# One kernel, two stored orders: attention and a SwiGLU layer on one core, with spare matmuls in other waits

## The chip, the cores and the metric

The kernel runs on one core of a Trainium2 chip. A core has five engines with a queue of instructions each: TensorE (PE, matrix products), VectorE (DVE), ScalarE (ACT), GpSimd (POOL) and SyncE (SP, which here only issues transfers). They run side by side and wait for each other through semaphores; transfers (DMAs) are issued from the queues of SP, ACT and POOL. Matrix products go to PSUM, a small memory that DVE and ACT read, and that POOL doesn't; everything else that is at hand lies in SBUF. The metric is the time of one execution in microseconds, the median of several runs.

## The reference

Attention with a forgetting factor, and a feed-forward layer (FFN) on its output:

```python
scores = scale * np.matmul(q, k.transpose(0, 1, 3, 2))        # 8 batches, 8 heads, 576 tokens, 64 wide
log_f = np.log(np.clip(f, 0.0001, 1.0))
cum = np.cumsum(log_f, axis=-1)
decay = cum[:, :, :, None] - cum[:, :, None, :]
scores = np.where(causal, -1000000000.0, scores + decay)
attn = softmax(scores)                                        # with 1e-09 in the divisor
x = np.matmul(attn, v)                                        # -> 4608 tokens x 512
xn = x / np.sqrt(np.mean(x * x, -1) + 1e-06) * rms_g
g, val = xn @ w_gate, xn @ w_val                              # 512 -> 1536, twice
out = (g * sigmoid(g) * val) @ w_out                          # 1536 -> 512, float32
```

The decay is split into a factor of the query, which the softmax's division removes, and one of the key, exp(-cum), by which the kernel scales the rows of V and a column of ones beside them.

## The kernel before, in words

**Pieces.** The program is cut into 1,551 pieces. Each has a name, an engine, a function that emits its instructions, and the pieces and buffers that it needs. A stored string, ORDER, lists the names; `plan.run` emits the pieces in exactly this order. So ORDER fixes two things: the order of the instructions in each engine's queue (an engine executes its own queue strictly in order, so a piece that waits holds up all that stand behind it on that engine), and which buffer a piece gets when it takes one, since a buffer must have been released by a piece that stands earlier. A word in ORDER may carry marks: `@A`, `@D`, `@O`, `@S` put the piece on ACT, DVE, POOL or SP where there is a choice, `:ff` takes a product's PSUM buffer from the FFN's pool, and `*n` asks for n spare matmuls ahead of the piece.

**Spare matmuls.** They multiply a zeroed 128x128 tile, `idle`, with itself, into the PSUM buffer that the piece has just taken and is about to overwrite. They wait for that buffer, and for nothing that the piece reads. Their result is never used:

```python
def warm_up(ps):                                   # L248 to L253
    k = st.pop("fill", 0)
    for w in [4] * (k // 4) + [1] * (k % 4):
        ...
        nc.tensor.matmul(ps[:, 0:w * 128], lhsT=idle, rhs=x, start=True, stop=True)
```

Score banks with masked blocks are opened by a piece of their own, `far`, which writes large negative numbers where a key lies behind the query; the score piece that follows finds the bank open:

```python
sc = T["sc", b, p, c0] if ("sc", b, p, c0) in T else open_sc(p, c0)    # scores(); open_sc calls warm_up
st.pop("fill", 0)
```

**Stages.** For each batch b: `L` pieces load q, k and v in pieces of 256 KB (Lq0.1 is the second part of batch 0's q; Lqk00 and Lqk01 are the last 64 tokens of q and k, half a piece each; Lv0.40 and Lv0.41 those of v, a quarter each), from SP's queue or ACT's. `C` pieces cast q and k to bfloat16 on POOL, ACT or DVE (L222). For batches 0 to 2 PE turns them (`tr`, `trt`, into a PSUM buffer of the FFN's pool, L528 to L558), and `keeptr` copies move them into QK or QT on DVE or ACT; for the later batches a transposing DMA on SP's queue does it (`tk`, `tq`, `tt`, L592 and L595). `S` pieces scale V by the decay (L451 to L458), which waits for `keep_dec`, the copy of the decay factors. Then for each pair p of heads: score banks (`sc`, L679; batch 0 has smaller banks than the others, and the masked ones begin with `far`, L664), exponentials on ACT (`esc`, L688), masks on POOL (L694), products with V (`val`, L714), division on DVE (`xpo`, L721 and L722). `sc4`, `exp4` and `mask4` are the last 64 keys. Row sums of squares on ACT (`sq`, L729), the inverse root on POOL (`rs`, L735), the norm on DVE (`xn`, L739), and a transpose of x on PE for batches 0 and 1 (`xtr`, L766), by DMA on SP's queue for the others (`tx`, L758).

**FFN.** The 4,608 tokens form ten groups, two of 256 and eight of 512. For each group and each 128 of the 1,536 columns PE computes a gate product (`g`) and a value product (`v..f`), four matmuls each (L863); ACT takes tanh of the gate (`th`, L868), DVE joins them in two steps (`ga` L872, `hga` L879). The output product (`pj`, L889) is copied out (`o`, L222) and stored (`so`, L897) from POOL's, SP's or ACT's queue. The FFN of earlier tokens is interleaved with the attention of later ones, so that PE has work while ACT computes exponentials.

**Buffers.** PSUM has two score banks ("sc"), one product buffer ("po") and three for everything else ("ff"). Ten staging buffers hold loads until they are cast.

**The front.** Weights are cast while they are loaded, from POOL's queue (`wg0` to `wv2`, L381; `wo`, L393). ORDER begins with constants, the log and the running sum of f, batch 0's loads and the first spare matmuls, and comes to the first FFN product, g0.0, after some 180 pieces.

Of the kernel before, what the change touches and what calls it, by code (L numbers as in the profile page):

```python
# [26 lines left out]
Cq1.0 Lv0.3 keeptr0.10.k Cqk0@D far0.2.0 keeptr0.10.q sc0.2.0 Lk1.3@A Sv0.0@O trt0 esc0.2.0 Lv0.41 keeptrt0 wv0 sc0.1.1024*6 Cqk1@A val0.0.0 Lk1.2
val0.4.0:ff keep_rg val0.6.0:ff xpo0.0.0 k4.0 Lk1.1 esc0.1.1024 val0.2.0:ff sc0.0.384 Lq1.2 wg0 xpo0.2.0 esc0.1.384 Lq1.1 sc4.0 xpo0.4.0 wg1 exp4.0
xpo0.6.0 esc0.3.384 far0.3.1024*4 esc0.0.384 Ck1.0 esc0.2.384 sc0.3.1024 Sv0.2 sq0.0 sc0.1.512 Lv1.41 trt1 esc0.3.1024 keeptrt1 Lv1.40 Sv0.3@O
esc0.1.512 Lqk20 sc0.0.512*9 Sv0.4 Lqk21 sq0.1 far0.0.1024*2 wv1 sc0.0.1024 esc0.0.512 rs0.0 Lk2.0 esc0.0.1024 sc0.2.512*6 tr1.0 mask4.0 xn0.1  # L30
far0.2.1024 keeptr1.0.q@A k4.1 Lv1.0 sc0.2.1024 esc0.2.512 keeptr1.0.k@D val0.0.2 val0.1.2:ff xpo0.0.2 esc0.2.1024 sc0.3.512 Cq1.2@O xpo0.1.2 val0.2.2
xn0.0 Ck1.1 esc0.3.512 val0.5.2:ff val0.3.2:ff xpo0.5.2 xtr0.0 wg2 sc1.0.512 Cq1.1@A kxtr0.0 xpo0.3.2 esc1.0.512 xtr0.1 Cq1.3 val0.4.2:ff xpo0.2.2
val0.6.2:ff wv2 Lq2.0 xpo0.4.2 kxtr0.1 val0.7.2 xpo0.6.2 Ck1.3@O tr1.1 esc1.0.0 xpo0.7.2 sc4.1 Ck1.2 g0.0 Lv1.3 keeptr1.1.k@D sq0.2 keeptr1.1.q v0.0f
th0.0 sq0.3 ga0.0 g0.2 exp4.1 sq0.4 hga0.0 sc1.0.1024 th0.2 rs0.2 tr1.3 esc1.1.512 ga0.2 xn0.2 v0.2f*4 keeptr1.3.q@A keeptr1.3.k@D esc1.0.1024 g0.4
# [931 lines left out]
```

## Time and profile before

| what | value |
|---|---|
| median of 7 runs | 384.2 us (380.27 to 385.13) |
| profiled execution | 384.62 us, its span 382.9 us |
| PE busy | 365.5 us, 95% of the span |
| DVE, ACT, POOL busy | 260.6, 220.7, 136.2 us |
| chain that ended last, by engine | PE 72%, DMA 8%, issue 6%, DVE 5%, ACT 4%, POOL 3% |
| granted TensorE clock | 0.50 from 21.80 to 28.63 us, 1.00 otherwise |
| first FFN product | 36.97 us |

Busy time of PE is the union of its matmuls' spans, whose ends are modelled, so 95% busy isn't 95% of what PE could do. The span counts from the first instruction to the last; the execution's time has some 1.7 us more. The granted clock is the share of the full clock that the chip's throttle let through; the profile names the stretches.

### The profile page before, as it was taken

The page shows a single profiled execution, that of the slowest core. Times are in us where ns is not written, and L with a number is a line of the kernel's source. Part 1 is how long each engine was busy: PE and PEld are TensorE (multiplying, and loading weights), DVE is VectorE, ACT ScalarE, POOL GpSimd, SP SyncE. Part 2 cuts the span into 40 slices and gives each one's busy share as a digit, 9 for nine tenths or more (in the row PEclk, how much of TensorE's full clock was granted, in tenths as well). Part 3 has the DMA queues.
Part 4 walks back from the last instruction along what each step waited for, and adds up shares of the span by engine and source line. Part 5 has one row for each costly group of instructions (what it writes and reads, how often), then busy time and mean ns, then how long its engine had stood idle before and what let it go on. Part 6 is the DMA issues. An engine that isn't in the chain of part 4 may idle for free.

```text
span 382.9 us, 8139 instructions
## 1 busy us (share of the span) xinstructions
PE 365.5 (95%) x3103; PEld 195.0 (51%) x3144; DVE 260.6 (68%) x497; ACT 220.7 (58%) x369; POOL 136.2 (36%) x249
## 2 busy tenths in 40 slices
PE   7679999999999899999899999999999999999996
PEld 3447788553644544455454544454445544444443
DVE  4648888778867778668757765778467876763560
ACT  5578978578697477544755587346565422323311
POOL 3566293237368144623531564020830111000001
PEclk9969999999999999999999999999999999999999
DMA  9999999697699799979969994641400234002002
GB/s 216 245 249 216 237 197 211 119 230 135 139 229 174 176 172 166 213 153 156 169 160 188 147 198 108 138 99 41 76 35 9 64 82 124 3 0 82 29 0 110
DMA packets 144774, 52.58 MB, mean 137 GB/s; under 512 B 128188, under 2 KB 141120, under 8 KB 144736
## 3 DMA queue, kind: packets, MB, share of 16 engines
q1 hardware_dynamic: 126992, 37.64, 52.1%
q0 software_dynamic: 6016, 8.79, 10.9%
q10 hardware_dynamic: 11728, 5.65, 6.2%
q8 instruction: 24, 0.39, 0.5%
q14 instruction: 14, 0.11, 0.1%
HBM read 37.90 MB, written 9.44 MB: 124 GB/s over the span
## 4 chain that ended last, share of the span: by engine, by line
PE 72%; DMA 8%; issue 6%; DVE 5%; ACT 4%; POOL 3%; SPq 1%; POOLq 0%; ACTq 0%; DVEq 0%
PE ff L863 42%; PE ff L889 18%; DMA st<-in_q_dram 5%; PE sc L679 4%; PE po L714 3%; DMA QK<-ld 2%; DVE xn L739 1%; DMA out_dram<-ores 1%; ACT PT L688 1%; PE ff L714 1%; POOL PT L694 1%; DVE X L722 1%; POOL rs L735 1%; ACT th L868 1%; ACT junk L729 1%
## 5 line engine op out<-in xcount | busy, mean ns | idle before, releaser
L868 ACT ACTIVATE th<-ff 128x512 f32<-128x512 f32 x108 | 64.5, 598 | 92.9 <-PE ff L863 88.2
L863 PE MATMUL ff<-xT,wv 128*128 128x512 bf16 (+1 forms) x466 | 109.7, 357 | 1.5 <-DVE ga L872 0.8
L863 PE MATMUL ff<-xT,wg 128*128 128x512 bf16 (+1 forms) x464 | 109.3, 357 | 0.8
L688 ACT ACTIVATE PT<-sc 128x1024 bf16<-128x1024 f32 (+2 forms) x100 | 96.4, 991 | 15.7 <-PE sc L679 13.8
L872 DVE SCALAR_TENSOR_TENSOR ga<-th,ff 128x512 f32<-128x512 f32 x108 | 74.0, 686 | 42.0 <-ACT th L868 41.5
L889 PE MATMUL ff<-wo,hT 128*128 128x512 bf16 (+1 forms) x433 | 97.4, 373 | 0.8 <-issue 0.2
L879 DVE SCALAR_TENSOR_TENSOR hT<-ga,ff 128x512 bf16<-128x512 f32 x108 | 73.7, 685 | 15.1 <-PE ff L863 6.4
L694 POOL TENSOR_SCALAR_AFFINE_SELECT PT<-PT 128x256 bf16<-128x256 bf16 (+1 forms) x84 | 42.1, 525 | 75.0 <-ACT PT L688 74.8
L863 PEld LDWEIGHTS <-wg 128*128 128x128 bf16 x480 | 45.2, 98 | 43.7 <-issue 1.9
L863 PEld LDWEIGHTS <-wv 128*128 128x128 bf16 x480 | 44.6, 98 | 43.9 <-issue 3.7
L889 PEld LDWEIGHTS <-hT 128*128 128x128 bf16 x444 | 42.3, 98 | 47.7 <-issue 1.4
L714 PEld LDWEIGHTS <-PT 128*128 128x128 bf16 x896 | 33.6, 98 | 12.5 <-issue 3.9
L739 DVE SCALAR_TENSOR_TENSOR xn<-X,rs,rgb 128x512 bf16<-128x512 f32 x40 | 33.9, 870 | 8.9 <-POOL rs L735 8.8
L222 ACT COPY ores<-ff 128x512 f32<-128x512 f32 (+1 forms) x25 | 14.2, 569 | 33.5 <-PE ff L889 27.6
L897 POOL DMA_DIRECT2D out_dram<-ores x16 | 9.2, 578 | 68.2 <-ACT ores L222 36.0
L222 POOL CAST ld<-st 128x512 bf16<-128x512 f32 x34 | 21.2, 631 | 29.0 <-DMA st<-in_k_dram 15.0
L679 PE MATMUL sc<-QK 64*128 64x256 bf16 (+3 forms) x272 | 28.6, 297 | 1.1 <-ACT QK L222 1.0
L735 POOL TENSOR_TENSOR rs<-sq,mhalf 128x5 f32<-128x5 f32 (+2 forms) x9 | 9.9, 1105 | 50.5 <-ACT junk L729 50.5
L729 ACT ACTIVATE junk<-X 128x513 bf16<-128x513 f32 x40 | 25.4, 635 | 3.9 <-DVE X L722 3.4
L451 POOL TENSOR_TENSOR Vs<-st,decT 128x512 bf16<-128x512 f32 x22 | 23.8, 1083 | 8.2 <-DMA st<-in_v_dram 7.6
L714 PE MATMUL po<-Vs,PT 128*128 128x65 bf16 x571 | 24.3, 194 | 0.1
L679 PEld LDWEIGHTS <-QK 64*128 64x128 bf16 x528 | 13.7, 96 | 19.8 <-issue 12.9
(90 smaller groups left out, 258.8 us busy)
## 6 DMA issues: line engine op xcount, KB each, us to landing
st<-in_k_dram SPq DMA_DIRECT2D x30, 256.0 KB, 4.5
st<-in_q_dram SPq DMA_DIRECT2D x29, 256.0 KB, 4.5
st<-in_v_dram SPq DMA_DIRECT2D x26, 256.0 KB, 4.5
out_dram<-ores POOLq DMA_DIRECT2D x15, 256.0 KB, 3.3
out_dram<-ores SPq DMA_DIRECT2D x12, 256.0 KB, 2.4
out_dram<-ores ACTq DMA_DIRECT2D x8, 256.0 KB, 2.5
st<-in_v_dram ACTq DMA_DIRECT2D x6, 256.0 KB, 4.4
wo<-in_moe_w_out_dram POOLq DMA_DIRECT2D x2, 768.0 KB, 9.7
```

Source lines behind the costliest of these rows:

```text
L222: {"DVE": nc.vector.tensor_copy, "POOL": nc.gpsimd.tensor_copy, "ACT": nc.scalar.copy}[eng](o, x)
L679: nc.tensor.matmul(sc[:, par, c:c + n], lhsT=k_cols(r, p, kj), rhs=q_cols(r, p, q0, n), start=not opened, stop=not opened or (kj, q0) == b ...
L688: nc.scalar.activation(T["pt", b, p][:, :, c0:c0 + n], T.pop(("sc", b, p, c0))[:, :, 0:n], ACT.Exp, scale=scale)
L694: nc.gpsimd.affine_select(out=d, in_=d, pattern=[[0, n], [1, 128]], compare_op=ALU.is_ge, fill=0.0, base=0, channel_multiplier=-1)
L714: nc.tensor.matmul(T["po", b, hs][:, qm, m, :], lhsT=w, rhs=Vs[i][:, kj, h, :], start=(kj == 0), stop=(kj == qi))
L729: nc.scalar.activation(junkp.tile([128, DM + 1], BF16, name="junk"), X[i][:, j, :], ACT.Square, scale=DM ** -0.5, accum_out=T["sq", b, js] ...
L739: nc.vector.scalar_tensor_tensor(xn, in0=X[i][:, j, 0:DM], scalar=T["rs", b, js][:, j:j + 1], in1=rgb, op0=ALU.mult, op1=ALU.mult)
L863: nc.tensor.matmul(ps[:, c * w:c * w + w], lhsT=wt[:, dc, (fc + c) * 128:(fc + c + 1) * 128], rhs=T["xT", g][:, dc, 0:w], start=(dc == 0), ...
L868: nc.scalar.activation(t, T["pg", g, fc], ACT.Tanh, scale=0.5)
L872: nc.vector.scalar_tensor_tensor(a, in0=T.pop(("th", g, fc)), scalar=1.0, in1=T.pop(("pg", g, fc)), op0=ALU.add, op1=ALU.mult)
L879: nc.vector.scalar_tensor_tensor(o, in0=T.pop(("ga", g, fc)).rearrange("p (c t) -> p c t", t=w), scalar=0.5, in1=T.pop(("pv", g, fc)).rear ...
L889: nc.tensor.matmul(po, lhsT=T["hT", g][:, fc, j * 128:(j + 1) * 128], rhs=wo[:, fc, c0:c1], start=(fc == 0), stop=(fc == NFC - 1))
```

## The change

ORDER is replaced by another list of the same 1,551 pieces. No function is touched, and all that is computed is the same. 134 pieces stand on another engine or queue than before (casts, copies, V's scaling, loads and stores), and the order of every queue differs from the first load on; PE's queue has the same piece at the same place in 169 of 459 places, and its last 22 pieces are the same. The counts behind a `*` are at twelve words in place of eight: trt0*84, tr0.00*44, sc0.1.0*4, far0.0.0*2, val0.0.0*16, sc0.3.512*12, far0.3.1024*4, val0.6.2*3, tr1.2*4, v0.0f*2, tr1.3*3 and v0.2f*2, where there were tr0.01*72, tr0.10*2, sc0.1.1024*6, far0.3.1024*4, sc0.0.512*9, far0.0.1024*2, sc0.2.512*6 and v0.2f*4.

The diff, cut to the front, to the stretch around batch 5's scores, and to the last lines:

```diff
 ORDER = """
-one lf far Lq1.0 Lq0.0 Lq0.1@A ident Lk0.0 Lv0.1@A tri identb clear Lk0.1 Lq0.3@A fetch_ln rg Lk0.2 clip Lk0.3@A log Cq0.1@A scan Lq0.2 Cq0.0@A Lqk01
-fetch Lv0.0 Ck0.0 tr0.01*72 Lqk11@A far0.1.0 keeptr0.01.q tr0.00 keeptr0.01.k far0.3.0 expo keeptr0.00.q sc0.1.0 Ck0.1@D Cq0.3@A twice keeptr0.00.k@D
-tr0.02 Lv0.40 turn_dec esc0.1.0 Lk1.0 tr0.03 turn_rg Ck0.2@O Lqk00@A far0.0.0 keeptr0.03.q keep_rgT keeptr0.03.k sc0.0.0 Lqk10@A Ck0.3 sc0.3.0
-keeptr0.02.k tr0.12 esc0.3.0 keep_dec Lq1.3 Cq0.2 keeptr0.02.q Sv0.1@O Lv0.2@A tr0.10*2 keeptr0.12.q far0.1.1024 esc0.0.0 keeptr0.12.k@D spread_rg
-Cq1.0 Lv0.3 keeptr0.10.k Cqk0@D far0.2.0 keeptr0.10.q sc0.2.0 Lk1.3@A Sv0.0@O trt0 esc0.2.0 Lv0.41 keeptrt0 wv0 sc0.1.1024*6 Cqk1@A val0.0.0 Lk1.2
-val0.4.0:ff keep_rg val0.6.0:ff xpo0.0.0 k4.0 Lk1.1 esc0.1.1024 val0.2.0:ff sc0.0.384 Lq1.2 wg0 xpo0.2.0 esc0.1.384 Lq1.1 sc4.0 xpo0.4.0 wg1 exp4.0
-xpo0.6.0 esc0.3.384 far0.3.1024*4 esc0.0.384 Ck1.0 esc0.2.384 sc0.3.1024 Sv0.2 sq0.0 sc0.1.512 Lv1.41 trt1 esc0.3.1024 keeptrt1 Lv1.40 Sv0.3@O
-esc0.1.512 Lqk20 sc0.0.512*9 Sv0.4 Lqk21 sq0.1 far0.0.1024*2 wv1 sc0.0.1024 esc0.0.512 rs0.0 Lk2.0 esc0.0.1024 sc0.2.512*6 tr1.0 mask4.0 xn0.1
-far0.2.1024 keeptr1.0.q@A k4.1 Lv1.0 sc0.2.1024 esc0.2.512 keeptr1.0.k@D val0.0.2 val0.1.2:ff xpo0.0.2 esc0.2.1024 sc0.3.512 Cq1.2@O xpo0.1.2 val0.2.2
-xn0.0 Ck1.1 esc0.3.512 val0.5.2:ff val0.3.2:ff xpo0.5.2 xtr0.0 wg2 sc1.0.512 Cq1.1@A kxtr0.0 xpo0.3.2 esc1.0.512 xtr0.1 Cq1.3 val0.4.2:ff xpo0.2.2
-val0.6.2:ff wv2 Lq2.0 xpo0.4.2 kxtr0.1 val0.7.2 xpo0.6.2 Ck1.3@O tr1.1 esc1.0.0 xpo0.7.2 sc4.1 Ck1.2 g0.0 Lv1.3 keeptr1.1.k@D sq0.2 keeptr1.1.q v0.0f
-th0.0 sq0.3 ga0.0 g0.2 exp4.1 sq0.4 hga0.0 sc1.0.1024 th0.2 rs0.2 tr1.3 esc1.1.512 ga0.2 xn0.2 v0.2f*4 keeptr1.3.q@A keeptr1.3.k@D esc1.0.1024 g0.4
...
-msc4.0.1024 Sv5.1@D sc4.2.1024 Lqk60 o3.1.0 pj3.2.0 Ck5.3@A so2.2.0@A tk5.3 so3.0.0@A esc4.2.1024 Lqk61 pj3.2.0e val4.3.0 tq5.1 esc4.3.512 pj3.3.0
...
-ga4.2 sc4.5 val4.2.0 th4.3 Lv7.41 hga4.2 v4.3f exp4.5 Lq6.3 ga4.3 mask4.5 g4.4 Lq6.2 Sv5.2 hga4.3 v4.4f Lv5.0 th4.4 xpo4.2.0 Ck5.2 ga4.4 g4.5 tk5.2
-hga4.4 sc5.0.512 th4.5 val4.6.0 esc5.0.512 ga4.5 Lv5.41 val4.7.0:ff xpo4.6.0 Lk6.0 v4.5f esc5.0.0 Cq6.2 tx3.2.5 g4.6 hga4.5 xpo4.7.0 val4.0.0 Sv5.0
-tq6.2 th4.6 v4.6f ga4.6 Sv5.4 g4.7 tt6 hga4.6 val4.4.0:ff xpo4.0.0 th4.7 sc5.0.1024 Ck6.3 Lq6.0 xpo4.4.0 esc5.0.1024 v4.7f Lk6.1 ga4.7 sq4.0 xn3.3
...
-th9.9 ga9.9 g9.10 hga9.9 v9.10f th9.10 ga9.10 g9.11 hga9.10 v9.11f th9.11 ga9.11 pj9.0.0 hga9.11 pj9.0.0e pj9.1.0 o9.0.0@D so9.0.0@O pj9.1.0e pj9.2.0
-o9.1.0 so9.1.0 pj9.2.0e pj9.3.0 o9.2.0 so9.2.0@O pj9.3.0e pj9.3.256 o9.3.0 so9.3.0@O pj9.3.256e o9.3.256 so9.3.256
...
+one lf rg Lq1.0 clear Lqk01 Lqk00@A tri Lk0.1 Lk0.0@A Lv0.40 Lk0.2@A ident fetch_ln Lq0.0 clip Cq1.0@D Lq0.2@A identb log Lq0.1 Cqk0 fetch Lq0.3 far
+trt0*84 Lv0.0 Ck0.0@D Lk0.3@A scan keeptrt0@A Lv0.3 k4.0@D expo Cq0.0@D Ck0.2 tr0.00*44 Lv0.1@A Cq0.2 turn_rg sc4.0 tr0.01 keeptr0.00.k@D Lk1.3 exp4.0
+far0.1.0 Ck0.1@D keeptr0.00.q@A keep_rgT Lqk10 twice keeptr0.01.k Cq0.1 keeptr0.01.q tr0.10 Ck0.3 tr0.03 keeptr0.10.q@A sc0.1.0*4 Lv0.2 Cq0.3@D
+keeptr0.03.q@A turn_dec esc0.1.0 keeptr0.03.k sc0.0.512 keep_dec Lk1.0@A tr0.02 tr0.12 Lv0.41 keeptr0.02.q esc0.0.512 far0.3.0 sc0.3.0 Lv1.41 Sv0.0
+keeptr0.02.k@A far0.2.0 esc0.3.0 Sv0.1 sc0.2.0 esc0.2.0 Lq1.3 far0.0.0*2 Sv0.3@O keeptr0.12.k@D sc0.0.0 Lqk11 keeptr0.10.k far0.1.1024 keeptr0.12.q@A
+wg1 Lq1.2 sc0.1.1024 esc0.0.0 val0.2.0 val0.4.0:ff Lv1.40 mask4.0 xpo0.4.0 esc0.1.1024 val0.0.0:ff*16 wg0 sc0.1.512 xpo0.0.0 val0.6.0:ff esc0.1.512
+xpo0.2.0 Ck1.0 sc0.0.384 spread_rg xpo0.6.0 esc0.1.384 esc0.3.384 Lq1.1 Sv0.2@O far0.0.1024 esc0.2.384 keep_rg@D Lk1.1 sq0.0 sc0.0.1024 tr1.0 Sv0.4
+Lk1.2 sq0.1 wv0 Lqk20 esc0.0.384 rs0.0 esc0.0.1024 sc0.3.512*12 Lk2.1 esc0.3.512 Cqk1 far0.3.1024*4 xn0.1 wv1 trt1 Lk2.0 sc0.3.1024 Lqk21 val0.0.2
+xn0.0 esc0.3.1024 sc0.2.512 keeptr1.0.k@D val0.1.2:ff esc0.2.512 far0.2.1024 Sv1.4 xpo0.1.2 sc0.2.1024 keeptrt1 val0.7.2:ff esc0.2.1024 keeptr1.0.q
+xtr0.1 kxtr0.1@D wg2 val0.6.2:ff*3 Lv1.2 Ck1.3@A xpo0.0.2 sc1.0.512 xpo0.7.2 k4.1 val0.2.2 esc1.0.0 xpo0.6.2 val0.3.2:ff wv2 xpo0.2.2 xtr0.0
+val0.5.2:ff esc1.0.512 Lq2.0 kxtr0.0 Ck1.1 val0.4.2 xpo0.5.2 g0.0 Cq1.1@A xpo0.3.2 Cq1.2@A Cq1.3@D tr1.1 xpo0.4.2 th0.0 Lq2.1 Ck1.2 sq0.3 ga0.0
+tr1.2*4 keeptr1.1.k keeptr1.1.q sc4.1 v0.0f*2 sq0.2 keeptr1.2.q sq0.4 g0.2 keeptr1.2.k@D Lv1.3 exp4.1 hga0.0 rs0.2 tr1.3*3 th0.2 sc1.0.1024 xn0.3
...
+xpo4.3.0 esc4.3.1024 v4.0f k4.5 ga4.0 tq5.1 val4.5.0 xpo4.1.0 Sv5.1 g4.1 xpo4.5.0 tk5.2 v4.1f hga4.0 msc4.3.1024 th4.1 Ck5.3@A ga4.1 sc4.5 g4.2 Cqk6@A
+Sv5.0 hga4.1 tk5.3 v4.2f th4.2 ga4.2 val4.2.0 Lq6.3 g4.3 hga4.2 Lv7.1 v4.3f xpo4.2.0 th4.3 Lv5.41 ga4.3 g4.4 Lv6.41 xn3.3 tt6 v4.4f th4.4 hga4.3
+exp4.5 val4.7.0 ga4.4 mask4.5 Lk6.0 g4.5 so3.3.0 hga4.4 tx3.2.5 v4.5f xpo4.7.0 th4.5 so3.2.0@A ga4.5 g4.6 Lv5.40 hga4.5 Lk6.1 v4.6f th4.6 Lk7.0 ga4.6
+sc5.0.512 Lk7.1 val4.4.0 esc5.0.0 hga4.6 val4.0.0:ff xpo4.4.0 g4.7 tx3.3.5 esc5.0.512 val4.6.0 th4.7 Lv6.1 sc5.0.1024 ga4.7 esc5.0.1024 v4.7f xpo4.0.0
+esc5.1.512 g4.8 xpo4.6.0 msc5.0.1024 hga4.7 v4.8f th4.8 Sv5.4 sq4.3 ga4.8 g4.9 hga4.8 sc5.1.0 th4.9 Sv6.3 Lv6.2 v4.9f esc5.1.0 ga4.9 Ck7.1 Cq6.3@D
...
+g9.10 hga9.9 v9.10f th9.10 ga9.10 g9.11 hga9.10 v9.11f th9.11 so7.0.0@A ga9.11 pj9.0.0 hga9.11 pj9.0.0e pj9.1.0 o9.0.0@D so9.0.0@O so8.3.0 pj9.1.0e
+pj9.2.0 o9.1.0 so9.1.0 pj9.2.0e pj9.3.0 o9.2.0 so9.2.0 pj9.3.0e pj9.3.256 o9.3.0 so9.3.0 pj9.3.256e o9.3.256 so9.3.256
 """
```

## The prediction

> **What bounds the kernel now.** I read the page's busy shares and its slices first, then the chain of waits up to 45 us, then the same stretch cut at the edges of the clock, and last PE's own idle times over the whole span.
>
> ```profile
> span 382.9 us, 8139 instructions
> ...
> PE 365.5 (95%) x3103; PEld 195.0 (51%) x3144; DVE 260.6 (68%) x497; ACT 220.7 (58%) x369; POOL 136.2 (36%) x249
> ...
> PE   7679999999999899999899999999999999999996
> ...
> PEclk9969999999999999999999999999999999999999
> ```
>
> PE is the bound: it is busy for 95% of the span, and 17.4 us are idle. The digits say where: in the first three slices (up to 28.7 us), and nowhere else by more than a tenth. The clock row has its only dent, a 6, in the third slice. A new order doesn't change what PE must compute, so it can only move those two things, and the few gaps behind them.
>
> The answer for PE's timeline has every gap; these five are the largest after 12 us:
>
> ```profile
> 17.89 0.40 PE L558 MATMUL ff<-ident,ld 128*128 128x128 bf16 x4 [1.43 <-DVE ld L222]
> 21.50 0.34 PE L714 MATMUL ff<-Vs,PT 128*128 128x65 bf16 x6 [1.63 <-ACT rgb L222]
> 94.79 1.02 PE L863 MATMUL ff<-xT,wv 128*128 128x512 bf16 x3 [0.61 <-DVE ga L872]
> 126.40 0.58 PE L714 MATMUL ff<-Vs,PT 128*128 128x65 bf16 x14 [0.80 <-ACT ores L222]
> 183.59 0.23 PE L679 MATMUL sc<-QT,QK 64*128 64x64 bf16 x4 [1.18 <-DMA QK<-ld]
> ```
>
> The number in brackets is PE's idle time before that row and who ended it. Behind 45 us only 2.6 us of single gaps are left. Busy time per stretch, cut at the clock's own edges (the columns are PE, PEld, DVE, ACT, POOL busy with counts, granted clock, DMA share, GB/s):
>
> ```profile
> 14.97:18.39 3.42, 1.89 (x20) 1.31 (x19) 1.86 (x5) 1.96 (x3) 3.18 (x6) 1.00 1.22 249
> 18.39:21.80 3.41, 1.35 (x34) 1.05 (x35) 0.98 (x4) 1.46 (x3) 2.83 (x5) 1.00 1.30 227
> 21.80:25.21 3.41, 2.89 (x39) 1.78 (x37) 2.46 (x8) 2.90 (x9) 2.38 (x3) 0.50 1.26 268
> 25.21:28.63 3.42, 3.27 (x21) 1.43 (x17) 1.50 (x6) 3.19 (x5) 0.92 (x2) 0.50 1.24 246
> ```
>
> After a stretch with 1.35 of 3.41 us busy (40%) the clock is granted at 0.50 for 6.83 us; after one with 1.89 (55%) it wasn't. Then the chain, where that half clock is paid:
>
> ```profile
> 13.36 6.92 DMA st<-in_q_dram
> ...
> 23.27 0.59 PE sc L253
> 23.85 0.64 PE sc L664 x4
> 24.49 0.56 PE sc L679 x6
> ...
> 26.15 1.12 PE sc L253 x3
> 27.27 0.54 PE sc L679 x4
> ```
>
> Until 20.28 us the end hangs on loads, here the q half of batch 1's tail, because its cast stands in ACT's queue ahead of the copy that frees a PSUM buffer (the 1.63 us gap). Then it hangs on matmuls at half clock, spare ones (L253) among them.
>
> **The change, part by part.** The profiled execution took 384.62 us, 1.7 us more than its span and 0.4 over the median of 384.2 of the seven runs; the sum is made against it. All 1,551 pieces stay, and 459 are PE's in both orders; 134 pieces change engine or queue (DVE +6, ACT +1, POOL -7). That is at most 6 x 0.69 = 4 us more on DVE, which idles 122 us: I cost it at nothing, covered by PE's 95%.
>
> *Spare matmuls.* A count of k stands for k//4 matmuls of 512 columns and k%4 of 128. But a count on a masked score bank does nothing: far_first (L664) has opened the tile, and scores drops the count. So sc0.1.1024*6 before and sc0.1.0*4 after are empty, and eleven waits get 53 matmuls (176 units of 128 columns) where seven got 30 (99 units). In the trace one of 512 columns takes 0.425 us at the cold start (loads of idle at 3.20, 3.63, 4.05) and 0.20 us later (eight in 1.61). The first group of 84 (21 matmuls) starts at 1.09, needs 9 x 0.425 up to 4.8 and 12 x 0.20 more: done at 7.3, as before (18 until 6.93). The other 92 units cost 23 x 0.20 = 4.6 us of PE. Under a real wait that is free; with no wait under them it is all on PE's path. Ends: 0 and +4.6. I take 0, since waits of that size are worked out below for the two largest groups, and the rest (20 units after those of 44, 16 and 12) is 1.0 us in seven places.
>
> *The loads come first in another sequence.* Now the tail of q and k and half of v's are loaded ahead of batch 0's rows. Ahead of the first pair's two operands (k0.0, q0.0) lie 1.79 MB: f's 0.15, Lq1.0, two tail halves, k0.1, k0.0, a quarter of v, k0.2, q0.0. Before it was 1.20 MB. At the 250 GB/s of 5 to 20 us (272, 242, 237 by stretch) that is 2.4 us later. Before, the first cast of k0.0 ran at 8.08 (POOL) and the turn at 8.74; so after at about 10.5 and 11. Under it stand trt0 (operands in by 6.5, runs at 7.3) and 44 spare units, 2.2 us, until 9.9: covered. Next in DVE's queue Ck0.3 stands ahead of keeptr0.03.k, Cq0.3, keep_dec and keeptr0.02.q. Its load is the 13th: 3.1 MB, by the same rate moved at 13.7 and, as k0.0 landed 1.4 us behind that count (7.94 against 6.5), landed at 15.1. With four pieces of 0.42 to 0.48 us, keep_dec ends near 17 (14.33 before), then Sv0.0 and Sv0.1 on DVE (0.80 + 0.20 each): the first value products at 19 to 20, against 19.15. ACT's exponentials of the head (0.81 each) are about 1 us later than before by then, and esc0.1.1024 ends near 22.4, against 22.2. So loading in this sequence costs 0.2 us at that point: the 2.4 us are absorbed, since before the same place waited for the tail's cast until 20.28, and that cast (Cqk1) is on POOL now.
>
> *From there to the first FFN product* (g0.0, 36.97 before). Three floors. ACT: before it did 10.32 us of work in the 11.60 from 22.20 to 33.80, where the last exponential of batch 0 ended; after, exp4.0 (0.38) and one bank (1.0) are already done, one row sum is added: 9.1 left, so 31.5 with ACT never idle and 32.8 with the same 1.3 idle. PE: the chain's matmuls from 22.43 to 28.63 are 0.38 + 0.59 + 0.64 + 0.56 + 1.12 + 0.54 + 0.33 + 0.49 = 4.65 us at half clock; at full clock 2.3 less, so 31.5 too. Does the clock hold? In the new order PE has, from 11 us on, tr0.00, turn_rg, sc4.0, tr0.01, far, tr0.10, tr0.03, sc0.1.0, turn_dec, sc0.0.512, tr0.02 (4.3 us by their rows) without a load to wait for, one wait of about 1.2 us for k0.3, and then four far and score pairs; no 3.41 us stretch falls to 1.35. I take that it holds, and 32.2, the middle of the two ACT ends: **-1.6 us**. From there before needed 3.17 to g0.0; after has two PE pieces less in that stretch (tr1.1 0.62, sc4.1 0.28), which come later: no gain. Ends of this part: -3.4 (all of 6.83/2) and +2.9 (second rival).
>
> At the first gap that matters the Trainium skill speaks against the change: its page "TensorE: Matmul & The Clock Gate", section "Why this matters for your kernels", says that gaps below some 3 us between bursts do no harm. This trace disagrees: its longest gap before 21.80 is 1.63 us, and the clock fell. By the page's rule the spare matmuls buy no clock, and the sum would be 383.4; by the rows it is the one below.
>
> *Behind the head.* The 1.18 us at 183.59: sc5.0.1024 waits for the transposing load of tk5.2, issued at 177.69, landed 5.85 us later. Between the two stand one score piece, four value products and four FFN products: 0.5 + 4 x 0.5 + 4 x 0.87 = 6.0 us of PE work. In the new order it is 13, and from tk5.3 to sc5.0.512 8.8: the wait goes, **-1.2 us**, nothing else there is late. The shortest such distance after is 5.0 (batch 3; 6.2 before), at a landing of 3.4 us in the median: covered, 1 us if it lands like the worst. Nearest distances from the last x transpose to its FFN group are 2.8 to 5.4 (2.8 to 6.1 before): as before. The gaps of 0.61 and 0.80 I leave standing: each hangs on a buffer's release whose place moves by a few pieces; ends -1.4 and +1.4.
>
> *Tail.* PE's last 22 pieces are the same. so9.2.0 and so9.3.0 move from POOL to SP: three stores on SP at 377.6, 378.7 and 380.0, 1.1 us or more apart, each 0.37 to 0.61 to issue: 0.
>
> Sum: 384.6 - 1.6 - 1.2 = **381.8**.
>
> **Rivals.**
> *The clock's loss comes back whole.* If PE is the bound from 21.80 on and ACT's idle time closes as well, the half clock cost 6.83/2 = 3.4 us: 384.6 - 3.4 - 1.2 = 380.0. For it: the seven times lie between 380.3 and 385.1, and a loss that some executions have and others don't would spread them so. Against it: ACT was busy 89% of the half-clock stretch. Chance 0.27.
> *The late front isn't made up (slower).* DVE's queue behind Ck0.3 holds keep_dec, and with it every Vs and value product. If k0.3 lands later than 17.3 (2.2 us later than my count), Sv0.1 ends past 21.5, where before PE went on, and from there each us is one on g0.0. At the full 2.4 us of the loads, with the spare groups of 16 and 12 (28 units, 1.4 us) then behind waits that are elsewhere: 384.6 + 2.4 + 1.4 = 388.4. For it: the first turn must be later. Chance 0.17.
> *The clock drops all the same.* The order moves the gap, for example to the wait for k0.3 and the 44 units end too early. Then only the later gap goes: 383.4, up to 385 with one new gap. Chance 0.13.
> The forecast itself has 0.43.
>
> **How the numbers follow.** A difference below 1% (3.8 us) is about what a measurement of this kernel can't tell from none: the seven runs spread by 4.9. Faster by 1% means below 380.4: two thirds of the first rival (0.18) and the third of the forecast in which the two gaps go as well (0.14): 0.32. Slower means over 388.0: most of the second rival, 0.15. The range leaves out a tenth on each side: down to 379.0 (the first rival less the gaps' lower end by 1.0), up to 388.0.
>
> **What would show it.** Right: PEclk without a 6 in slices two to four; the first batch-0 turn at about 11; exponentials of batch 0 over by 32 to 33; g0.0 near 35; no wait for QK's DMA near 180. Wrong: a 0.50 clock anywhere after 5 us; g0.0 past 37; L253 rows in the chain with a full clock (spare matmuls on the path); or gaps behind 45 us that add to more than 2.6 us, which a count of distances in the order can't exclude.

## The result

The changed kernel takes 384.85 us (median of 25 runs, 383.17 to 386.93), the kernel before 382.53 us (median of 62, 380.00 to 385.13). The ratio is 1.0062, with a 95% interval from 1.0047 to 1.0078: **slower by 0.6%, 2.3 us**, where 381.8 us and a gain were forecast. It is inside the 1% that the prediction called too small to tell from no change, but with this many runs the sign is sure. The profiled execution of the changed kernel took 384.34 us, so it stands near its median; that of the kernel before took 384.62 us, 2.1 us above its own.

The page of the changed kernel, the lines that answer to those shown of before:

```profile
span 382.2 us, 8187 instructions
...
PE 368.7 (96%) x3125; PEld 194.8 (51%) x3167; DVE 260.6 (68%) x502; ACT 221.0 (58%) x370; POOL 130.1 (34%) x241
...
PE   8789999999999999989999999899999999999996
...
PEclk9999999999999999999999999999999999999999
```

The dent in the clock row is gone, PE is busy for 3.2 us more than before. Its busy row has one digit more in each of the first three slices, no 8 any more at 124 and 181 us, and new ones at 162 and 239 us. Busy time per stretch of the changed kernel, at the same edges as shown for before (columns: PE, PEld, DVE, ACT, POOL busy with counts, granted clock, DMA share, GB/s):

```profile
14.97:18.39 3.42, 2.70 (x36) 1.77 (x34) 3.08 (x6) 2.75 (x4) 1.50 (x2) 1.00 1.29 228
18.39:21.80 3.41, 2.97 (x38) 1.60 (x38) 2.90 (x7) 2.47 (x5) 2.38 (x4) 1.00 1.26 219
21.80:25.21 3.41, 3.14 (x56) 2.29 (x57) 2.64 (x9) 3.41 (x8) 2.50 (x4) 1.00 1.24 212
25.21:28.63 3.42, 2.35 (x27) 1.13 (x25) 2.27 (x5) 2.98 (x6) 2.06 (x3) 1.00 1.25 240
```

Where before had 1.35 us busy and then 6.83 us at 0.50, the changed order has 2.97 and a clock of 1.00. In its 26 executions the mean clock was never below 0.998; in the 95 of the kernel before whose clock is on record it lay between 0.982 and 0.996. So the change does what the forecast took from it, and is slower all the same. PE's timeline of the changed kernel shows by what (the number in brackets is PE's idle time before the row, and who ended it; rows with L253 are spare matmuls):

```profile
20.52 1.02 PE L253 MATMUL ff<-idle 128*128 128x512 bf16 x4
22.07 0.35 PE L714 MATMUL ff<-Vs,PT 128*128 128x65 bf16 x6 [0.52 <-ACT PT L688]
...
26.34 0.81 PE L253 MATMUL sc<-idle 128*128 128x512 bf16 x3 [1.07 <-ACT PT L688]
...
27.41 0.39 PE L253 MATMUL sc<-idle 128*128 128x512 bf16 x1
...
37.12 0.27 PE L253 MATMUL ff<-idle 128*128 128x128 bf16 x2 [0.34 <-DVE ga L872]
...
39.40 0.34 PE L253 MATMUL ff<-idle 128*128 128x128 bf16 x3 [0.17 <-DVE QK L222]
...
41.35 0.27 PE L253 MATMUL ff<-idle 128*128 128x128 bf16 x2 [0.28 <-ACT QK L222]
...
168.43 0.29 PE L630 MATMUL sc<-QT,K 128*128 128x64 bf16 x4 [0.76 <-POOL K L222]
...
244.52 1.02 PE L863 MATMUL ff<-xT,wg 128*128 128x512 bf16 x4 [0.92 <-DVE ga L872]
```

Two kinds of spare group can be told apart. The one at 20.52 (of 16) runs *before* an idle time of 0.52 us that ends with data: it fills a wait. Those at 26.34, 37.12, 39.40 and 41.35 run *after* the idle time. They write the PSUM buffer that their piece has taken, so they wait for it too; where the wait was for that buffer, nothing is left to fill, and they stand between the buffer's release and the work. (The group at 27.41 has no wait ahead of it, since the one at 26.34 has used it up.) The chain of waits of the same kernel, up to 45 us, has them, at full clock:

```profile
26.02 0.28 ACT PT L688
26.34 0.81 PE sc L253 x3
...
27.47 0.32 PE sc L253
...
31.55 0.33 PE ff L253 x3
...
39.40 0.34 PE ff L253 x3
...
41.35 0.27 PE ff L253 x2
```

The other two rows, at 168.43 and 244.52, are new waits behind the front. For the first, POOL's timeline has the copy that PE waits for:

```profile
167.53 0.84 POOL L222 COPY K<-QT 64x256 bf16<-64x256 bf16 x2 [4.16 <-DMA QT<-ld]
```

It is k4.5, two copies, on POOL now (0.84 us for both) instead of DVE (0.21 and 0.22), and it waits for the transposing load of tt5, issued at 162.32 and landed at about 167.5. From the gate product g4.0, which stands behind tt5 in both orders, to sc4.5 lay 7.6 us of PE work in the old order, and 5.0 in the new one (by the costs given below). For the second, ACT's timeline (an ACTq row is ACT's queue issuing a transfer):

```profile
240.56 1.02 ACT L688 ACTIVATE PT<-sc 128x1024 bf16<-128x1024 f32 x1 [0.88 <-PE sc L679]
242.77 0.34 ACTq L897 DMA_DIRECT2D out_dram<-ores  x1
243.15 0.60 ACT L868 ACTIVATE th<-ff 128x512 f32<-128x512 f32 x1 [1.56 <-DMA xT<-xn]
```

The store so5.2.0 stands in ACT's queue ahead of the tanh th6.0. It isn't issued before 242.77, 0.08 us after the transposing load tx5.2.7, issued on SP's queue at 237.22, has landed at 242.69; th6.0 stands behind it, ACT idles for 1.56 us, and PE for 0.92 us. The trace also says what held the store. The copy that it stores had ended at 240.35, but ahead of the store ACT's queue has an instruction that waits for semaphore 114 until 242.73: tx5.2.7's landing raises that semaphore, and the store's own landing is told by the same one. So the wait came from the program, which gave both transfers one semaphore. A store on ACT's queue in the middle of the FFN is thus on the path when it must wait.

To see how much each place costs, I compare times of single tanhs (one per FFN product) less the PE work that stands ahead of them in that order, each piece by the mean of its row (0.87 us for four FFN matmuls, 0.5 for a value product, a score piece or a turn, 2.4 for an output product, and so on). Only differences of this number mean something:

| up to | after less profiled before (384.62) | after less before once more (382.64) |
|---|---|---|
| th0.0, first tanh | -1.65 us | -0.90 us |
| th0.4 | -0.20 | +0.55 |
| th4.0 | -1.73 | -0.73 |
| th4.3, behind the wait at 168 | -1.21 | +0.25 |
| th6.3, behind the wait at 244 | -0.89 | +1.10 |
| th9.11, last tanh | -1.03 | +0.94 |
| time of the execution | -0.28 | +1.70 |

The right column has an execution of before close to its median (the first experiment). Against it the new order is early at the first tanh, late four products later, gains until th4.0, and loses again at both new waits. The last 0.75 us come behind the last tanh.

### The profile page after: what moved, and what is told of

Same layout as the page of the kernel before. It is cut to its first block, busy times and chain, and to the rows that moved or that the text cites. A ratio compares the mean times of both kernels' runs of the same rounds, so it can differ in the third digit from the quotient of the medians.

```text
span 382.2 us, 8187 instructions
## 1 busy us (share of the span) xinstructions
PE 368.7 (96%) x3125; PEld 194.8 (51%) x3167; DVE 260.6 (68%) x502; ACT 221.0 (58%) x370; POOL 130.1 (34%) x241
## 4 chain that ended last, share of the span: by engine, by line
PE 76%; DMA 6%; DVE 5%; ACT 5%; issue 3%; POOL 3%; SPq 1%; ACTq 0%; POOLq 0%; DVEq 0%
PE ff L863 43%; PE ff L889 19%; PE sc L679 5%; PE po L714 4%; DMA st<-in_k_dram 3%; PE ff L714 2%; ACT PT L688 2%; DMA xT<-xn 1%; DMA st<-in_v_dram 1%; DVE QK L222 1%; POOL Vs L451 1%; ACT QK L222 1%; DVE ga L872 1%; SPq L592 1%; PE ff L528 1%
## 5 line engine op out<-in xcount | busy, mean ns | idle before, releaser
L688 ACT ACTIVATE PT<-sc 128x1024 bf16<-128x1024 f32 (+2 forms) x100 | 95.2, 990 | 15.1 <-PE sc L679 14.9
L739 DVE SCALAR_TENSOR_TENSOR xn<-X,rs,rgb 128x512 bf16<-128x512 f32 x40 | 30.6, 790 | 13.7 <-POOL rs L735 13.7
L897 POOL DMA_DIRECT2D out_dram<-ores x14 | 8.2, 589 | 70.0 <-DVE ores L222 62.4
L222 ACT COPY ores<-ff 128x512 f32<-128x512 f32 (+1 forms) x20 | 11.3, 564 | 34.6 <-PE ff L889 30.3
L222 POOL CAST ld<-st 128x512 bf16<-128x512 f32 x30 | 18.7, 629 | 28.8 <-PE ff L863 8.0
L451 POOL TENSOR_TENSOR Vs<-st,decT 128x512 bf16<-128x512 f32 x22 | 22.9, 1043 | 9.7 <-DMA st<-in_v_dram 6.2
```

Of the source, the lines that this page charges most:

```text
L222: {"DVE": nc.vector.tensor_copy, "POOL": nc.gpsimd.tensor_copy, "ACT": nc.scalar.copy}[eng](o, x)
L451: e.tensor_tensor(Vs[i][:, j, :, 0:D], t, bcast(dj, D), ALU.mult)
L688: nc.scalar.activation(T["pt", b, p][:, :, c0:c0 + n], T.pop(("sc", b, p, c0))[:, :, 0:n], ACT.Exp, scale=scale)
L739: nc.vector.scalar_tensor_tensor(xn, in0=X[i][:, j, 0:DM], scalar=T["rs", b, js][:, j:j + 1], in1=rgb, op0=ALU.mult, op1=ALU.mult)
```

## Experiments

**The kernel before once more.** Nothing is edited; its 384.62 us lay high, and the question was what a usual execution looks like.

> The kernel before once more, for a second profile: its profiled execution took 384.62 us, but the median of many is 382.5. Theory 1 (the clock): the executions differ by how long the half clock lasts, since the clock's stretches of 3.41 us lie elsewhere against the program each time. A profile near 382.5 us then shows a half-clock stretch shorter than 6.83 us or none, and the first FFN product about 2 us earlier than 36.97. Theory 2 (transfers): the clock's dent is the same 6.83 us, and the time differs behind the front, in the 1.18 us gap near 184 us and its like.

Measured: 382.64 us. The half clock is there and as long as in the first profile (6.83 us), but 1.25 us earlier, from 20.55 to 27.38; th0.0 comes 0.75 us earlier (37.30), and the gaps of 0.61, 0.80 and 1.18 us are 0.32, 0.53 and 0.65. So a usual execution doesn't lack the half clock (none of the 95 has a mean clock over 0.996): of the 2.0 us between the two, 0.75 is the front and 1.1 is those three gaps.

**Only the two large groups** (84 and 44).

```diff
...
-far0.0.0*2
+far0.0.0
...
-val0.0.0:ff*16
+val0.0.0:ff
...
-sc0.3.512*12
+sc0.3.512
...
-far0.3.1024*4
+far0.3.1024
...
-val0.6.2:ff*3
+val0.6.2:ff
...
-tr1.2*4
+tr1.2
...
-v0.0f*2
+v0.0f
...
-tr1.3*3
+tr1.3
...
-v0.2f*2
+v0.2f
...
```

> The new order with only its first two groups of spare matmuls (84 ahead of trt0, 44 ahead of tr0.00); the ten other counts are taken off. Theory 1 (the small groups stand behind a wait for the buffer that they write, so they come after the wait and are PE time on its path): in the profile of the new order 0.11 + 0.65 + 0.22 + 0.16 + 0.21 + 0.11 + 0.18 + 0.11 us of them follow such a wait or have none, 1.75 us in all, so 383.1 us, 1.7 below the new order's 384.85. Theory 2 (they keep the clock): without them the clock falls to 0.50 somewhere before 35 us and the time is 385 to 387. Theory 3 (neither): 384.85 within 0.5.

Measured: 383.44 us (381.25 to 385.29), ratio 1.0022 (0.9994 to 1.0050). The half clock came back in each of the 12 runs (mean clock 0.990 to 0.996), and still the median is 1.4 us below the change's, near the first expectation; the two intervals just overlap, so this alone doesn't make it certain. If it holds, the 48 units taken out cost more than the clock that they held. In its trace the waits at 168 and 244 us aren't there, though nobody touched them: PE comes later here (th0.4 at 45.31 instead of 43.41), so the gains of different edits need not add.

**The old front with the new rest, and the other way round.** The pieces ahead of g2.0 in one order, then all that remain, in the sequence of the other.

```diff
-one lf rg Lq1.0 clear Lqk01 Lqk00@A tri Lk0.1 Lk0.0@A Lv0.40 Lk0.2@A ident fetch_ln Lq0.0 clip Cq1.0@D Lq0.2@A identb log Lq0.1 Cqk0 fetch Lq0.3 far
+one lf far Lq1.0 Lq0.0 Lq0.1@A ident Lk0.0 Lv0.1@A tri identb clear Lk0.1 Lq0.3@A fetch_ln rg Lk0.2 clip Lk0.3@A log Cq0.1@A scan Lq0.2 Cq0.0@A Lqk01
...
+Lv2.41@A kxtr1.0 Lk3.1 xtr1.4 keeptr2.2.q Lq3.1 Cq3.1@A tq3.1 Lv2.2@A Ck3.1 Lv2.40 tk3.1 so1.0.0 kxtr1.4 Lv4.40 Sv2.4 keeptr2.2.k g2.0 Ck3.3@A v2.0f
...
```

> The old order up to g2.0 (some 70 us), with its own spare matmuls, then the remaining pieces in the new order. Theory 1 (the new order loses in its front): about the time of before less the gap at 184 us, 381 to 382.5. Theory 2 (it loses behind the front or in its tail): 384 to 385, as the new order.

> The new order up to g2.0, with its spare matmuls, then the remaining pieces in the old order: the counterpart. Theory 1 (the loss is in the front): 384.5 to 386. Theory 2 (behind it or in the tail): 381.5 to 383, the old time or a little below it.

Measured: 385.57 us (ratio 1.0074, 1.0043 to 1.0105) and 386.63 us (1.0100, 1.0064 to 1.0135). Both are slower than either parent, since the seam itself costs: PE idles for 2.14 and 0.72 us at 86.8 and 88.5 us in the first, 2.65 us at 87.7 in the second, where no parent waits. Less the seam (3.1 to 3.3 us and some 2.4 at th2.0, by the same reckoning as in the table) they would be near 382.3 and 384.2; at th2.3 the seam has cost 4.5 and 3.5 us, with a half clock from 87.93 to 91.34 in the first, and they would be near 381.1 and 383.1. Both lean to the front as the place of the loss. But sums that need a correction larger than the effect settle nothing.

**The two waits mended**, all spare groups kept: sc4.5 moved behind v4.2f, and the store so5.2.0 behind th6.0 and esc6.2.1024.

```diff
...
-sc4.5
...
+sc4.5
 th4.2
...
-so5.2.0@A
...
 esc6.2.1024
+so5.2.0@A
 ga6.0
...
```

> The new order with all its spare matmuls; two things are moved: sc4.5 stands two FFN products later in PE's queue (behind v4.2f), and the store so5.2.0 stands on ACT's queue behind th6.0 and esc6.2.1024 in place of ahead of th6.0. Theory 1 (the new order loses 0.76 us at 168 us where sc4.5 waits for k4.5, and 0.9 to 1.4 us at 243 us where a store in ACT's queue waits until 242.77 for a transposing load and holds up th6.0): 384.85 - 0.8 - 1.1 = 383.0. Theory 2 (PE's lead is spent at the next wait on another engine whatever these two are): 384.3 to 384.9, with new gaps in PE behind 170 us.

Measured: 383.87 us (382.68 to 385.83), ratio 1.0043 (1.0023 to 1.0064): 1.0 us less than the change, half of the 1.9 that was reckoned, and the two intervals overlap. The wait at 168 is gone. At the other place a neighbour comes in, as PE's timeline shows:

```profile
240.91 2.75 PE L889 MATMUL ff<-wo,hT 128*128 128x512 bf16 x11 [1.01 <-DVE ores L222]
```

**Both: two waits mended, only the two large groups.** The edits of the two kernels above, together; measured in two series, on two chips.

```diff
...
-val0.0.0:ff*16
+val0.0.0:ff
...
-sc0.3.512*12
+sc0.3.512
...
-sc4.5
...
+sc4.5
 th4.2
...
-so5.2.0@A
...
 esc6.2.1024
+so5.2.0@A
 ga6.0
...
```

> As the run before this, and only the groups of 84 and 44 spare matmuls are left. Theory 1 (small groups on PE's path, 1.75 us, and the two waits): 383.44, as with the two groups alone, less what is left of the two waits there; since PE came 0.5 to 1.9 us later to them in that profile and had no gap at either place, 383.0 to 383.4. Theory 2 (both gains add in full): 381.5.

> The changed order with the two waits mended and with only the groups of 84 and 44, once more, in the same call as the next kernel. Theory 1 (its 382.18 stands: the small groups and the two waits are what made the change slower): 382.2, ratio 0.998 to 1.000. Theory 2 (the order itself is slower, and that median came from a quiet call): 383 to 384, as with the kernels that differ from it in the last stores or in one group alone (382.9 and 384.0).

Measured: 382.18 us, ratio 0.9980 (0.9955 to 1.0006), and 380.93 us, ratio 0.9981 (0.9954 to 1.0009); 381.47 is the median of all 22 runs, as if both gains added in full (381.5 expected). With the groups in, the same order had a ratio of 1.0043 (1.0023 to 1.0064); the intervals don't meet, and the difference of 0.0062 is 2.4 us, 48 units of 0.05 (by the medians of the first series alone it is 1.7). The two profiled executions, both without a half clock in the front, differ by 0.82 us at th0.4, 1.24 at th2.3 and 1.64 at the end. So the spare groups cost time in this order. Neither series tells it from the kernel before for certain. Its PE timeline in the first series at the places of the largest groups:

```profile
26.76 0.39 PE L679 MATMUL sc<-QK 64*128 64x256 bf16 x4 [1.08 <-ACT PT L688]
27.68 0.49 PE L664 MATMUL sc<-far,ident 128*128 128x256 bf16 x4 [0.52 <-ACT PT L688]
...
39.27 0.62 PE L528 MATMUL ff<-ident,ld 128*128 128x128 bf16 x8 [0.17 <-DVE QK L222]
```

The waits of 1.08 and 0.17 us are as long without a spare group as the 1.07 and 0.17 us ahead of one in the change. Only the one of 0.52 us at 27.68 had been covered by the group in front.

**The old order with its first group alone** (72).

```diff
...
-tr0.10*2
+tr0.10
...
-far0.3.1024*4
+far0.3.1024
...
-sc0.0.512*9
+sc0.0.512
...
-far0.0.1024*2
+far0.0.1024
...
-sc0.2.512*6
+sc0.2.512
...
-v0.2f*4
+v0.2f
...
```

> The old order with its first group of 72 alone; six later groups (27 units of 128 columns) are off. Theory 1 (small groups are PE time on the path): in the chain of the profile before they took 0.59 + 1.12 + 0.33 + 0.43 us at half clock, so 382.5 - 1.5 to 2.5 = 380 to 381. Theory 2 (ACT sets the pace there, so that they fill time that is idle anyway): 382.5 within 0.7. Theory 3 (without them the half clock lasts one stretch of 3.41 us longer): 383.5 to 384.5.

Measured: 381.61 us (380.77 to 383.09), ratio 0.9988 (0.9970 to 1.0006). The clock is lower than ever (0.981 to 0.987; in its profile 3.41 and 6.83 us at 0.50), and it isn't slower. It lies between the first two expectations. The likely reading is that small groups cost time in the old order too, about as much as the clock that they save.

**The small groups doubled.** The eight groups of the change that stand behind a buffer's wait, 32 units, become 64.

```diff
...
-far0.0.0*2
+far0.0.0*4
...
-sc0.3.512*12
+sc0.3.512*24
...
-far0.3.1024*4
+far0.3.1024*8
...
-val0.6.2:ff*3
+val0.6.2:ff*6
...
-tr1.2*4
+tr1.2*8
...
-v0.0f*2
+v0.0f*4
...
-tr1.3*3
+tr1.3*6
...
-v0.2f*2
+v0.2f*4
...
```

> The changed order with eight of its spare groups doubled (the ones that in its trace stand behind a wait for a buffer: 12, 2, 4, 3, 4, 2, 3 and 2 units become 24, 4, 8, 6, 8, 4, 6 and 4); the groups of 84, 44 and 16 stay. Theory 1 (a spare matmul waits for the PSUM buffer that its piece has taken, so it stands behind such a wait and is PE time on the path): 32 more units at 0.05 us are 1.6 us, so 384.85 + 1.6 = 386.4, between 386.0 and 387.0. Theory 2 (the spare matmuls are covered by waits and cost nothing; the order alone is slower): 384.85 as before, between 384.3 and 385.4.

Measured: 385.39 us (four runs, 384.81 to 385.84), ratio 1.0087 (1.0061 to 1.0112), against 1.0062 for the change: the time is just inside the second expectation's range, and the intervals overlap, so the times don't decide. Its PE timeline says more:

```profile
26.59 1.46 PE L253 MATMUL sc<-idle 128*128 128x512 bf16 x6 [1.07 <-ACT PT L688]
...
40.68 0.50 PE L253 MATMUL ff<-idle 128*128 128x512 bf16 x3 [0.17 <-DVE QK L222]
```

The waits are again 1.07 and 0.17 us: twice the matmuls don't shorten them. Counted from the first turn of batch 0, the tanh th0.4 starts 30.61 us later with no small group, 31.43 with 48 units (32 of them behind a buffer's wait), and 32.60 with these doubled: 0.82 us for the first 32, of 1.6, and 1.17 for the next. Other kernels with this front have 31.50 and 31.86 with the 48 units, and 30.74 and 30.85 without (33.14 where a load came late, last section).

**The group of 16 put back** into the kernel with both edits.

```diff
...
-val0.0.0:ff
+val0.0.0:ff*16
...
```

> The changed order with the two waits mended and with the groups of 84, 44 and 16 (val0.0.0, where PE waits for data and not for the buffer). Theory 1 (only spare matmuls behind a buffer's wait cost time): 382.2, as with two groups, at most 0.3 more. Theory 2 (every spare matmul past the first two groups is PE time): 16 units at 0.05 us, 382.2 + 0.8 = 383.0.

Measured: 383.95 us (381.05 to 384.95), ratio 1.0038 (1.0014 to 1.0061), more than either theory allowed. In its trace the group is hidden: the value product behind it starts 10.08 us after the first turn, and 10.09 us without the group. A load of this execution came late, though, and the half clock fell from 29.14 to 32.55 (last section). The two executions at a clock of 0.998 took 381.05 and 381.29 us, but the one at 1.000 took 383.81. By the medians this one group would cost as much as all 48 units, so the medians don't tell which groups the price belongs to; that the groups behind a buffer's wait pay it is read from the traces. Why most of the others were late, also against the same kernel without the group at the same clock (384.1 against 382.1 us at 0.994 and 0.995), stays open. This kernel and the next were measured on another chip than the one without the group, and a part of that may be the chip's.

**The old stores at the end**, in the kernel with both edits.

```diff
...
+so7.0.0@A
...
+so8.3.0
...
-so7.0.0@A
...
-so8.3.0
...
-so9.2.0
+so9.2.0@O
...
-so9.3.0
+so9.3.0@O
...
```

> The changed order with the two waits mended and with only the groups of 84 and 44, and in it the stores of the end as in the old order: so9.2.0 and so9.3.0 on POOL's queue, so8.3.0 right behind o8.3.0, so7.0.0 behind so7.2.0. From the last tanh to the end of the time the old order takes 16.3 us, the changed one 16.9 to 17.0. Theory 1 (the stores' queues at the end cost that 0.7 us): 382.2 - 0.7 = 381.5, and us less span back at 1.7. Theory 2 (the end is late for another reason, such as what was issued long before): 382.2, us less span at 2.0 to 2.1.

Measured: 382.89 us (380.15 to 384.38), ratio 1.0025 (1.0005 to 1.0045): not the gain. The end itself did get shorter, in the profiled execution: 16.43 us from the last tanh to the end of the time, where the kernel with both edits has 16.94, the change 17.03 and the kernel before 16.28, and 1.16 us from the last store's landing to the end of the span instead of 1.52. So the stores' queues cost some 0.5 us there, by this pair of traces; but the kernels with one front and the other rest don't follow them (1.20 us with the new end, 1.69 with the old; 16.43 and 16.83 us from the last tanh), and the median rose. What else made this kernel slower is open.

**The old order with two more groups**, meant for waits for data.

```diff
...
-trt0
+trt0*24
...
-sc0.0.512*9
+sc0.0.512
...
-val0.0.0
+val0.0.0*16
...
```

(The other small groups are out, as in the kernel with the first group alone.)

> The old order with its first group of 72 and two groups in front of pieces that wait for data there, trt0*24 and val0.0.0*16; the other small groups are gone. With the first group alone it took 381.6 at a clock of 0.981 to 0.987. Theory 1 (within one order the clock costs what it takes, 2.5 to 3.8 us per 0.01): if the two groups bring the clock to 0.991, 380.0 to 380.5; if to 0.998, 377.5 to 379. Theory 2 (the clock is worth little here, since ACT works on at its own speed): 381.6 whatever the clock is. If the clock stays at 0.981 to 0.987, it tells nothing of this, and 40 units of 0.05 us in real waits should leave 381.6.

Measured: 382.43 us (380.08 to 384.71), ratio 1.0016 (0.9988 to 1.0044), and a clock that differs from run to run: four runs at 0.982 have a median of 384.2 us, four at 0.990 and 0.991 one of 382.4, three at 0.994 to 0.996 took 380.5 to 381.7, the one at 1.000 took 380.08. The slope is 2.2 us for 0.01 of clock (correlation -0.94), and 2.6 in the 95 runs of the kernel before (-0.55). So the theory that the time doesn't go with the clock is wrong: it does, with some 60 to 70% of what the clock takes (0.01 of 382 us is 3.8), if the loads that make both late (last section) have no share in it. That they may have one is seen in the other kernels with 7 to 12 runs, where the slope is anything from 1.1 (both edits, first series) to 5.6 (only the two large groups), the last more than the clock itself could take.

The trace shows that the second group didn't stand in a wait for data: neither in the profile before nor with the first group alone does PE wait ahead of val0.0.0. Three products further on it waits for an "ff" buffer, until ACT's copy into rgb frees it (1.63 and 1.07 us). The 16 units write the "po" buffer, take 0.87 us ahead of this, and no such wait of over 0.15 us is left. So a wait for a buffer can be filled, by a group that stands earlier and writes another one. The medians at a given clock are worse than with the first group alone; in the two profiled executions the first tanh comes 28.8 us after the first turn in both, and the first turn itself 0.85 us later (8.25 against 7.40), so the groups aren't shown to be the reason.

## Why the prediction was wrong

**The clock: right; its size is open.** That the new order holds it, the forecast's condition, is what the profile and all 26 executions show. From 0.991 to 1.000 it is worth 2.0 to 2.3 us by the slopes of the two old orders, against the forecast's 1.6 and the first rival's 3.4; by the slopes of the other kernels it could be anything from 1.0 to 5.1. The marks set for it also came: first turn at 11.98 (11 forecast), k0.3 landed at 15.29 (15.1), first value products at 20.14 (19 to 20), the last exponential of batch 0 over at 31.68 (32 to 33), g0.0 at 34.40 (35), no wait for a transposing load near 180.

**The first step that failed: "I take 0, since waits of that size" stand over the spare matmuls.** Such waits are there; but a spare matmul waits for the same PSUM buffer, so a wait that this buffer's release ends can't be filled by it. This was readable beforehand, in the function that emits them and in rows of before, where the spare matmuls follow the idle time:

```profile
23.27 0.59 PE L253 MATMUL sc<-idle 128*128 128x512 bf16 x1 [0.47 <-ACT P L634]
...
26.15 1.12 PE L253 MATMUL sc<-idle 128*128 128x512 bf16 x3 [0.15 <-ACT PT L688]
```

In the traces up to th0.4 it is 0.8 us for 32 units, in the medians up to 2.4 us for 48, with the group of 16 among them (its share isn't settled); the end of +4.6 us that the prediction kept for the range was on the right side. The row that it named as the mark of this, L253 in the chain at full clock, is there five times.

**The second: no wait was counted in the front between g0.0 and th0.4.** The turn tr1.1, which came before g0.0, and tr1.2, which came behind g0.4, stand between g0.0 and g0.4 now, beside tr1.3, and in this stretch PE waits 0.34, 0.17 and 0.28 us for DVE and ACT. The first tanh's 1.65 us lead on the profiled execution was down to 0.20 four products later. These 0.8 us and 0.6 us of spare matmuls between the two make up the difference, and the forecast's -1.6 is spent.

**The third: "nothing else there is late".** The gap of 1.18 us went as forecast, and those of 0.61 and 0.80 with it, 2.6 us together. In their place came 0.76 us at sc4.5 and 0.92 us at the products behind g6.0. The first would have been found by counting tt5's distance as tk5.2's was; the second is a store in ACT's queue, and ACT's queue wasn't walked for what waits in it. Mending both brought back 1.0 of the 1.7 us by the medians, with intervals that overlap. Between th0.4 and th6.3 the balance is -0.69 us on the profiled execution, near the -1.2 forecast; on a usual execution of before, whose three gaps had only 1.5 us, it is +0.55.

**The fourth: the tail at 0.** It costs 0.75 us (17.03 against 16.28 us from the last tanh), 0.36 of it between the last store's landing and the end of the span and 0.4 outside the span. One pair of traces ties 0.5 us to the stores' queues; the cause isn't settled.

**The base.** The sum was made against an execution of 384.62 us. Of the 2.0 us by which that lies above the second profile, 1.1 are the three gaps, and the forecast counted the one of 1.18 us as gained. It was 0.65 us in the second profile, 0.47 in the old order with two more groups, and with the first group alone it wasn't there. So about half of the -1.2 us or more was a property of one execution, and 381.8 would have been 0.7 us below the usual 382.5, not 2.8 below.

**Of the rivals**, the clock's loss coming back whole is wrong by a third of its size if the slopes of the old orders hold; the late front is wrong as to its mechanism (k0.3 landed 2 us ahead of the deciding point), though the spare groups behind the wrong waits that it counted on top, 1.4 us, are what happened. The sum of the losses with their ends, 0.8 to 2.4 + 0.8 + 1.7 + 0.75, is 4.0 to 5.6 us, against gains of 2.0 to 2.3 for the clock, by these slopes, and 1.5 for the gaps of a usual execution: +0.2 to +2.1 with the clock at that price, and more with a smaller one, where +2.3 was measured. So it closes only with the larger price of the spare groups, or a smaller one of the clock; which of the two isn't settled.

The Trainium skill was weighed in the prediction: against drops in the middle of a kernel its page "TensorE: Matmul & The Clock Gate", section "Why this matters for your kernels", asks for no idle gap of PE over some 3 us. The runs here show again that this isn't enough, with the clock lost at 22.23 us in an order whose longest gap there is 1.44 us.

## What to carry to other kernels

A filler that writes the buffer it waits for can't fill the wait for that buffer's release: before you add one, look in the trace for who ends the wait, and if it is that release, leave the filler out, or put it earlier and into another buffer. Set a forecast against several executions of the kernel before, since a gap that you remove may be one that most executions don't have. And when an order is replaced, walk every queue, ACT's with its stores included, for what stands behind an instruction that waits, also for a semaphore that two transfers share.

## What the runs showed of the hardware

**One load decides whether PE waits, and has a part in whether the clock falls.** The kernels of the changed order with the two large groups, waits mended or not, have the same instructions up to the first tanh, and the other kernels with this front differ from them there by spare matmuls alone. Yet one load, Lqk11, the second half of batch 1's last 64 tokens, lands 6.0 to 8.9 us after its issue:

| kernel | Lqk11 landed | PE's wait ahead of trt1 | half clock (3.41 us) from | first tanh after the first turn |
|---|---|---|---|---|
| both edits, second series | 24.54 us | none | 22.23 us | 23.46 us |
| both edits, old stores at the end | 25.26 | none | none | 23.35 |
| the change | 25.83 | none | none | 23.75 |
| both edits, first series | 26.62 | none | none | 23.21 |
| two waits mended, all groups | 27.07 | none | none | 23.83 |
| small groups doubled | 27.50 | none | none | 24.92 |
| new front, old rest | 27.61 | 0.10 us | none | 24.19 |
| both edits, three groups | 27.64 | 0.41 | 29.14 | 24.78 |
| only the two large groups | 28.06 | 1.06 | 28.86 | 25.74 |

In the last two kernels the cast on POOL waits for it, the turn trt1 on PE for the cast, and the half clock follows. At 27.61 us, in an order with all spare groups, PE's wait is 0.10 us and the clock holds, and the first kernel of the table lost the clock with the earliest landing of all. So the load alone doesn't decide the clock. In the last kernel of the table, POOL's timeline and PE's:

```profile
28.21 0.80 POOL L222 CAST ld<-st 128x512 bf16<-128x512 f32 x1 [1.12 <-DMA st<-in_k_dram]
```

```profile
29.07 0.61 PE L558 MATMUL ff<-ident,ld 128*128 128x128 bf16 x4 [1.06 <-POOL ld L222]
```

So a late load can make an execution longer and lower its clock too, and the time that goes with the clock from run to run need not be the clock's alone: of the 2.5 us between both edits' first series and the last row, 1.06 are that wait.

**The same 3.41 us of half clock cost almost nothing or about 1.5 us.** The first row of the table loses them and stands 0.25 us behind the first series of the same kernel; the last loses them and stands 1.5 us behind that beyond its wait. The stretches of these two, first row and then last (columns as above):

```profile
22.23:25.64 3.41, 3.41 (x44) 2.34 (x42) 2.33 (x8) 3.30 (x8) 2.03 (x4) 0.50 1.25 224
```

```profile
25.45:28.86 3.41, 0.96 (x10) 0.55 (x8) 2.26 (x6) 2.89 (x6) 1.38 (x2) 1.00 1.25 261
28.86:32.27 3.41, 3.21 (x41) 2.19 (x42) 0.28 (x1) 1.73 (x2) 2.26 (x6) 0.50 1.25 261
```

In the half-clock stretch of the first, ACT is busy for 3.30 of 3.41 us: it has hardly any time to lose, and PE's slowness is hidden. In that of the last ACT is busy for 1.73 us and DVE for 0.28, and ACT's waits that end there, 2.2 us in all, end with PE. So a lower clock need not mean a longer time. In the old order with its first group alone ACT is busy for 2.10, 3.41 and 2.67 us of the three stretches at half clock: hidden in one of them at most, by this measure.

**Whether the clock drops isn't read from the busy share alone.** It fell after stretches of 3.41 us with 0.96, 1.35, 1.52 and 1.96 us of busy PE, in the old order with its first group alone after 2.14 and 2.06, and not after one with 1.89 us in the kernel before or ones with 2.05 and 1.86 in the first series of both edits.
